# Half-size block products (Strassen's scheme) in the second MLP product of two batches

## The chip, the cores and the metric

The kernel runs on one core of a Trainium2 chip. A core has five engines with a queue of instructions each: TensorE (matrix products, PE in the profile; its weight loads are listed as PEld), VectorE (DVE), ScalarE (ACT), GpSimd (POOL) and SyncE (SP, which here only issues DMA transfers). The queues run side by side and wait for each other by semaphores. Operands lie in SBUF, matrix products arrive in PSUM, and DMA moves data from and to HBM. The metric is the device time in microseconds (us), as the median of several runs.

## The reference

The first half is block-sparse attention over 4 batches, 8 heads, 768 tokens and 64 numbers per head; a boolean mask by blocks of 32 tokens says which scores count. The second half mixes the tokens and ends in an MLP, both with residual paths:

```python
attn = softmax(where(mask, q @ k.T / 8, -1e9));  x = attn @ v      # then [b, 768, 512]
a1 = alpha1 * x + beta1
tok = np.einsum('ts,bsd->btd', w_tok, a1)
u = x + lam * tok
a2 = alpha2 * u + beta2
ch = np.maximum(a2 @ w_ch1, 0.0) @ w_ch2      # 512 -> 2048 -> 512
return u + lam * ch
```

The change concerns the product with `w_ch2`, 768 x 2048 by 2048 x 512 in each batch, and the addition after it.

## The kernel before, in words

The work is done in 16 pairs of heads, four to a batch. Tokens lie six to a partition, so a batch has six token tiles of 128, and `x_sbs[b]` (128 partitions x 6 x 512, float32, three buffers) holds a batch's attention output and later its residual sum `u`. `lam` is folded into the weights beforehand: into `w2b`, the bfloat16 copy of `w_ch2` (16 tiles of 128 rows, 512 columns), by the products on line 764.

PSUM has eight banks: two `sp` tiles of two banks each, three `mm` tiles of one bank, one `op` tile. Scores go to `sp` tiles or to two `mm` tiles (`emit_qk`, L582), ScalarE takes their exponential (`emit_exp`, L600), VectorE multiplies by the mask (`emit_keep`, L617), TensorE forms the products with the values in `op` (L629, L652), and VectorE divides by the row sums (`emit_finish`, L669 and L670). `emit_a1pp` (L686, L687) applies `alpha1` and `beta1`, on GpSimd, for a batch's last head on VectorE. For every two pairs of heads `job_tok2` mixes the tokens (three jobs of 12 matmuls, L826, each followed by the residual addition on L838 and two casts to `ubf` on L844). `emit_udma` transposes `ubf` by DMA, issued on SyncE, and `emit_uscale` (L877) writes `uT`, with `alpha2` and `beta2`, which is what the MLP reads.

The MLP has two kinds of jobs. `job_f1(b, c, n)` makes one 128-wide tile `n` of the 2048 hidden numbers for half `c` of a batch's tokens: four matmuls of 384 columns (L891) into an `mm` tile and a ReLU on ScalarE (L898) into `hts[(b, c)]`. There are 32 in a batch, and `hts` has two buffers. `job_f2(b, o, g)` is a quarter of the second product for token tile `o`: four matmuls of 512 columns (L910) into the `mm` tile `chs[(b, o)]`; the fourth quarter is followed by the addition of `x_sbs` on VectorE into a tile `ot` (L919) and by a store on SyncE's queue. The last token tile of the last batch is done apart, by `job_f2_cols` (matmuls on L930, additions on L938), in a part of 384 and one of 128 columns.

The order of the instructions on each engine is written out by hand. After 45 steps of a first loop, which follows the due times in `PLAN`, come rows of `WEAVE`, counted on from row 15, and each of their letters issues one thing: `q` the scores of three units and the first exponential, `x` a further exponential, `k` a mask product, `p` a group of value products, `0 1 2` what `PLAN` has for the three steps, `L` loads, `Q K Y` transposes and copies for the next pair, `s` the start of a finished pair, `T` one `job_tok2`, `d` one `emit_udma`, `v` one `emit_uscale`, `f` one `job_f1`, `g` one `job_f2`. The nine rows of `W1` are rows 15 to 23; the twelve rows of `W2` are used twice, as rows 24 to 35 and 36 to 47; the three rows of `W3` have no scores left and finish batches 2 and 3. A batch's second product is spread over the rows in which the next batch's scores are computed. Every engine takes its instructions in the order in which they were issued, so what is issued later on a queue waits for what stands before it there.

Of the kernel before, what the change touches and what calls it, by code (L numbers as in the profile page):

```python
# [25 lines left out]
DM = 512  # L26
P = 128
NT = S // P
NH = 4 * DM // P
# [13 lines left out]
W1 = [  # L43
# [9 lines left out]
]  # L53
W2 = [
# [12 lines left out]
]  # L67
W3 = [
# [3 lines left out]
]  # L72
WEAVE = W1 + W2 * (B - 2) + W3
ENG = {
    "kT0": 0,
    "kT1": 0,
# [153 lines left out]
def kernel(  # L230
# [16 lines left out]
    nc = tc.nc  # L247
# [22 lines left out]
    ap_ = ctx.enter_context(tc.tile_pool(name="attn", bufs=1))  # L270
# [4 lines left out]
    def ptile(shape, dt, name):  # L275
        return pp.tile(shape, dt, name=name, tag=name)
# [46 lines left out]
    qTs = [ptile([P, 2, S], BF, f"qTs{i}") for i in range(NQB // 2)]  # L323
    kTs = [ptile([P, 2, S], BF, f"kTs{i}") for i in range(NQB // 2)]
# [24 lines left out]
    for n, src in enumerate((moe_lam, moe_alpha1, moe_beta1)):  # L349
# [10 lines left out]
        out=identb[:],  # L360
# [33 lines left out]
    for o in (slice(0, 4), slice(4, NT)):  # L394
# [18 lines left out]
        out=mbs[0:NBLK, :],  # L413
        in0=mbm[0:NBLK, :],
# [27 lines left out]
    def sp_tile():  # L442
        return psum.tile([P, 2, 512], FP, name="sp", tag="sp", bufs=2)
# [6 lines left out]
    def mm_tile(shape=(P, DM), dt=FP):  # L450
        return psum.tile(list(shape), dt, name="mm", tag="mm", bufs=3)
# [103 lines left out]
    x_sbs = {}  # L555
# [142 lines left out]
    w2b = ptile([P, NH, DM], BF, "w2b")  # L698
# [94 lines left out]
    hts = {}  # L793
# [92 lines left out]
    def job_f1(b, c, n):  # L886
        if n == 0:
            hts[(b, c)] = ap_.tile([P, NH, QC], BF, name="hts", tag="hts", bufs=2)
        ps = mm_tile()
        for dk in range(4):  # L890
            nc.tensor.matmul(  # L891
                ps[:, 0:QC],
                w1b[:, dk, ts(n, P)],
                uTs[b][:, dk, ts(c, QC)],
                start=(dk == 0),
                stop=(dk == 3),
            )
        nc.scalar.activation(  # L898
            hts[(b, c)][:, n, :], ps[:, 0:QC], AF.Relu
        )  # L900

    chs = {}

    def job_f2(b, o, g):
        if g == 0:
            chs[(b, o)] = mm_tile()
        ps = chs[(b, o)]
        ht = hts[(b, o // 3)]
        for nk in range(4 * g, 4 * g + 4):
            nc.tensor.matmul(  # L910
                ps[:],
                ht[:, nk, ts(o % 3, P)],
                w2b[:, nk, :],
                start=(nk == 0),
                stop=(nk == NH - 1),
            )
        if g == 3:
            ot = ap_.tile([P, DM], FP, name="ot", tag="ot", bufs=3)
            nc.vector.tensor_tensor(  # L919
                out=ot[:], in0=x_sbs[b][:, o, :], in1=ps[:], op=ALU.add  # L920
            )
            nc.sync.dma_start(
                out[b].rearrange("(p o) n -> p o n", o=NT)[:, o, :], ot[:]
            )

    def job_f2_cols(b, o, sl):
        ps = mm_tile()
        ht = hts[(b, o // 3)]
        for nk in range(NH):
            nc.tensor.matmul(  # L930
                ps[:, sl],
                ht[:, nk, ts(o % 3, P)],
                w2b[:, nk, sl],
                start=(nk == 0),
                stop=(nk == NH - 1),
            )
        ot = ap_.tile([P, DM], FP, name="ot", tag="ot", bufs=3)
        nc.vector.tensor_tensor(  # L938
            out=ot[:, sl], in0=x_sbs[b][:, o, sl], in1=ps[:, sl], op=ALU.add
        )  # L940
        nc.sync.dma_start(
            out[b].rearrange("(p o) n -> p o n", o=NT)[:, o, sl], ot[:, sl]
        )

    NPAIR = B * NP
    WIDE = [
# [28 lines left out]
    ]  # L975
    N1 = MP * len(WIDE)
    LAG = 2
    todo = {"f": [], "g": [], "t": []}

    def start_mlp(b):  # L980
        todo["f"] += [
            lambda c=c, n=n: job_f1(b, c, n) for c in range(2) for n in range(NH)
        ]
        os_ = range(NT) if b < B - 1 else range(NT - 1)
        todo["g"] += [lambda o=o, g=g: job_f2(b, o, g) for o in os_ for g in range(4)]
# [112 lines left out]
    for s in range(N1):  # L1098
# [42 lines left out]
    def token(t, p):  # L1141
# [34 lines left out]
    assert not (todo["f"] or todo["g"] or todo["t"] or pend or kept)  # L1176
    for sl in (slice(0, 3 * P), slice(3 * P, DM)):
        job_f2_cols(B - 1, NT - 1, sl)
# [1 line left out]
_INS = ['q', 'k', 'v', 'sampled_blocks', 'moe_alpha1', 'moe_beta1', 'moe_w_tok', 'moe_alpha2', 'moe_beta2', 'moe_w_ch1', 'moe_w_ch2', 'moe_lam']  # L1180
_OUTS = [((4, 768, 512), 'float32')]
# [25 lines left out]
```

## Time and profile before

| | us |
|---|---|
| median of three runs (lowest to highest) | 302.34 (302.17 to 303.07) |
| span of the profiled execution, from its first to its last instruction | 300.1 |
| busy in it: TensorE / ScalarE / VectorE / GpSimd | 293.2 / 212.7 / 195.6 / 112.0 |
| ReLU products (L891, 512 matmuls) / second MLP product (L910, 343 recorded), busy | 92.6 / 84.4 |

The profile gives one execution; apart from its span no time of its own is listed, so the difference to the median, 2.2 us, lies around the span or between executions. Busy times of matmuls overlap in its groups, since one starts before the one before it has left the array: the mean length of one in a group is longer than the interval at which they follow each other. A row of a group reads: line, engine, operation, output <- inputs, partitions x elements and type, how many; then busy us and the mean in ns of one; then the idle time of the engine just before them and what ended most of it. A row of the timeline reads: start, length, engine, line, operation, and in square brackets a wait before it with what ended it. Rows of a line's instructions give shortest/mean/longest in ns and the time of the first and the last.

### The profile page before, as it was taken

To read this page: it belongs to the slowest core of one execution; us is meant where nothing else is said; L and a number is where in the kernel's file an instruction comes from. 1 tells how busy PE (TensorE), PEld (TensorE's weight loads), DVE (VectorE), ACT (ScalarE), POOL (GpSimd) and SP (SyncE) were. 2 spreads that over 40 slices of the span, in tenths; PEclk is the share of its full clock that TensorE was granted. 3 is DMA by queue.
4 is the path that set the end of the run, shared out by engine and by line. 5 is a ranking of instruction groups with operands and counts; after the bars stand their busy time and mean duration, and the time that the engine had idled before them with its cause. 6 is when DMAs were issued, how large, how long until landed. Compare 5 with 4: busy or idle time off the path is not lost.

```text
span 300.1 us, 7192 instructions
## 1 busy us (share of the span) xinstructions
PE 293.2 (98%) x2970; PEld 183.2 (61%) x2995; DVE 195.6 (65%) x374; ACT 212.7 (71%) x314; POOL 112.0 (37%) x151
## 2 busy tenths in 40 slices
PE   7999999999999999999999999999999999999996
PEld 2788888664577565555675565565576564555543
DVE  4979899985688796963669687972769672000012
ACT  5999999998899944998878763998779400673210
POOL 8997887632525700564315320362322200000000
PEclk9999999999999999999999999999999999999999
DMA  6999999951491993629835693629102004000011
GB/s 182 187 201 187 189 166 196 194 94 28 101 171 21 142 178 81 131 46 149 127 57 86 110 176 85 120 64 135 49 18 52 37 35 122 37 0 37 35 70 70
DMA packets 57929, 31.26 MB, mean 104 GB/s; under 512 B 37989, under 2 KB 54673, under 8 KB 57897
## 3 DMA queue, kind: packets, MB, share of 16 engines
q0 software_dynamic: 16752, 14.22, 33.1%
q1 hardware_dynamic: 40820, 16.19, 26.3%
q8 instruction: 23, 0.38, 0.5%
q10 hardware_dynamic: 324, 0.40, 0.5%
q14 instruction: 10, 0.07, 0.1%
HBM read 29.75 MB, written 6.29 MB: 120 GB/s over the span
## 4 chain that ended last, share of the span: by engine, by line
PE 94%; ACT 3%; DMA 1%; issue 1%; DVE 0%; ACTq 0%
PE mm L891 28%; PE mm L910 26%; PE sp L582 10%; PE op L652 9%; PE mm L826 8%; PE mm L582 4%; PE mm L802 3%; ACT eT L600 2%; PE op L629 2%; PE mm L629 1%; PE mm L930 1%; DMA ms<-ms_c 1%; PE mm L780 1%; PE mm L492 1%; PE mm L532 0%
## 5 line engine op out<-in xcount | busy, mean ns | idle before, releaser
L600 ACT ACTIVATE eT<-sp,expb 128x1024 f16<-128x1024 f32 x111 | 118.3, 1121 | 1.8 <-PE sp L582 1.1
L891 PE MATMUL mm<-uT,w1b 128*128 128x384 bf16 x512 | 92.6, 326 | 0.1
L898 ACT ACTIVATE hts<-mm 128x384 bf16<-128x384 f32 x128 | 60.9, 500 | 42.1 <-PE mm L891 41.5
L617 DVE TENSOR_TENSOR eT<-eT,mask 128x1024 f16<-128x1024 f16 x99 | 80.2, 840 | 15.9 <-ACT eT L600 15.7
L910 PE MATMUL mm<-w2b,hts 128*128 128x512 bf16 x343 | 84.4, 379 | 1.3 <-issue 0.3
L686 POOL TENSOR_TENSOR a1pp<-x_sb,vbc 128x384 bf16<-128x384 f32 x26 | 29.7, 1141 | 124.2 <-DVE x_sb L670 94.7
L891 PEld LDWEIGHTS <-w1b 128*128 128x128 bf16 x512 | 48.2, 98 | 33.3 <-issue 2.1
L600 ACT ACTIVATE eT<-mm,expb 128x512 f16<-128x512 f32 x66 | 41.8, 685 | 27.2 <-PE mm L582 26.8
L910 PEld LDWEIGHTS <-hts 128*128 128x128 bf16 x368 | 33.7, 98 | 38.4 <-issue 4.7
L919 DVE TENSOR_TENSOR ot<-x_sb,mm 128x512 f32<-128x512 f32 x23 | 15.8, 686 | 49.2 <-PE mm L910 41.8
L652 PEld LDWEIGHTS <-eT 128*128 128x128 f16 x792 | 29.9, 98 | 8.3 <-issue 1.3
L652 PE MATMUL op<-vext,eT 128*128 128x65 f16 x792 | 32.1, 194 | 0.2
L687 POOL TENSOR_TENSOR a1pp<-a1pp,vbc 128x384 bf16<-128x384 bf16 x26 | 27.7, 1065 | 2.1
L582 PE MATMUL sp<-qTs,kTs 88*128 88x512 bf16 (+1 forms) x120 | 26.9, 326 | 1.3 <-ACT kTs L432 0.8
L826 PE MATMUL mm<-a1pp,wtokT 128*128 128x256 bf16 x216 | 25.9, 273 | 0.0
L826 PEld LDWEIGHTS <-wtokT 128*128 128x128 bf16 x216 | 20.6, 98 | 5.5 <-issue 2.5
L582 PE MATMUL sp<-qhT,khT 64*128 64x256 bf16 (+1 forms) x176 | 19.7, 322 | 0.0
L838 DVE TENSOR_TENSOR x_sb<-x_sb,mm 128x512 f32<-128x512 f32 x18 | 12.3, 686 | 10.2 <-PE mm L826 10.1
L582 PEld LDWEIGHTS <-khT 64*128 64x128 bf16 x264 | 10.5, 94 | 12.2 <-issue 8.6
L629 PEld LDWEIGHTS <-eT 128*128 128x128 f16 x360 | 14.9, 97 | 3.8 <-issue 0.3
L670 DVE TENSOR_TENSOR x_sb<-op,rcp 128x384 f32<-128x384 f32 x28 | 15.6, 558 | 1.0
L844 DVE CAST ubf<-x_sb 128x256 bf16<-128x256 f32 (+1 forms) x44 | 13.7, 346 | 0.9
(94 smaller groups left out, 221.8 us busy)
## 6 DMA issues: line engine op xcount, KB each, us to landing
out_dram<-ot SPq DMA_DIRECT2D x23, 256.0 KB
qpad<-in_q_dram POOLq DMA_DIRECT2D x15, 192.0 KB, 4.8
kr<-in_k_dram POOLq DMA_DIRECT2D x15, 192.0 KB, 5.5
vr<-in_v_dram POOLq DMA_DIRECT2D x15, 192.0 KB, 6.1
w1b<-in_moe_w_ch_dram POOLq DMA_DIRECT2D x4, 512.0 KB, 9.1
w2b<-in_moe_w_ch_dram POOLq DMA_DIRECT2D x4, 512.0 KB, 8.1
hts<-in_moe_w_tok_dram POOLq DMA_DIRECT2D x2, 576.0 KB, 9.7
x_sb<-in_k_dram ACTq DMA_DIRECT2D x2, 192.0 KB
```

The lines of the kernel that those rows point to most:

```text
L582: nc.tensor.matmul(sp[jj][:, dst], lhsT, rhs, start=True, stop=True, skip_group_check=True,)
L600: nc.scalar.activation(dst, at, AF.Exp, bias=expb[:], scale=SCALE)
L617: nc.vector.tensor_mul(out=e, in0=e, in1=keep)
L629: nc.tensor.matmul(op[0][:, o, :], ets[u][:, jj, h * QB + n * P : h * QB + n * P + P], vexts[i % NVB][:, w, 2 * jp + jj, :], start=op[1] == 0,
L652: nc.tensor.matmul(op[0][:, o, :], ets[u][:, jj, h * QB + n * P : h * QB + n * P + P], vexts[i % NVB][:, w, 2 * jp + jj, :], start=op[1] == 0,
L686: eng.tensor_tensor(out=dst, in0=x_sbs[b][:, :, cols], in1=bc[0], op=ALU.mult)
L687: eng.tensor_tensor(out=dst, in0=dst, in1=bc[1], op=ALU.add)
L826: nc.tensor.matmul(ps[:, o], wtokT[:, os_, ts(2 * n + o, P)], a1pps[i][:, os_, :], start=(os_ == 0 and o == 0), stop=(os_ == NT - 1 and o ...
L891: nc.tensor.matmul(ps[:, 0:QC], w1b[:, dk, ts(n, P)], uTs[b][:, dk, ts(c, QC)], start=(dk == 0), stop=(dk == 3),)
L898: nc.scalar.activation(hts[(b, c)][:, n, :], ps[:, 0:QC], AF.Relu)
L910: nc.tensor.matmul(ps[:], ht[:, nk, ts(o % 3, P)], w2b[:, nk, :], start=(nk == 0), stop=(nk == NH - 1),)
L919: nc.vector.tensor_tensor(out=ot[:], in0=x_sbs[b][:, o, :], in1=ps[:], op=ALU.add)
```

## The change

In batches 2 and 3 (`STR`) the second product takes token tiles in pairs (t, t+3), t from 0 to 2, one from each half `hts[(b, 0)]` and `hts[(b, 1)]`. The 256 x 2048 by 2048 x 512 product is cut into two by two blocks: two token tiles by two halves of the hidden numbers (`HN` = 8 tiles each), and two halves of `w2b`'s rows by two halves of its columns (`HC` = 256). In the Strassen-Winograd form, four sums of blocks on each side give seven products instead of eight. Each product `job_p(b, t, n)` is 8 matmuls of 256 columns (L1052 of the changed file), 56 for a pair where there were 32 of 512.

The sums on the weights' side (`T1`, `T2`, `T4`, and a fourth written over `w2b`'s own upper right block) are formed once, by 16 instructions of 512 elements on GpSimd (`job_t`, letter `A`, L979); they lie in the four tiles `qTs` and `kTs`, which the later pairs of heads no longer use. The sums on the tokens' side (`job_s`, letter `S`, L1026) are formed for each pair: `X1` and `X2` into new tiles, two more over blocks of `hts`. In batch 2 numbers 1 and 2 run on VectorE and 3 and 4 on GpSimd; in batch 3, 1 to 3 run on VectorE and 4 on GpSimd.

The sums on the results' side are formed partly by accumulation in PSUM (products that go on in a bank in which an earlier one stands) and partly on VectorE, which adds a bank to `x_sb` in place (`plus`, L1062) after a product, sometimes to two blocks at once (`twice`). For a pair, products 6, 7, 5 and 4 use the two banks of one `sp` tile, and product 1 (batch 3) or 6 (batch 2) opens it; products 1, 2 and 3 use `mm` tiles as well. Stores now read `x_sb`, in batches 0 and 1 too, and the tile `ot` and `job_f2_cols` are gone; the last product of all is done in two parts of 128 columns.

Batch 2's products 1 and 2 of the three pairs stand in rows 42, 43 and 46; its products 6, 7, 5, 4, 3 follow from row 47 into `W3`. For that, two of batch 2's `f` are issued earlier (rows 43 and 44). In batch 3 all 32 `f` come first, with the upper and the lower half of the hidden tiles in turn, and its 21 products stand at the very end.

```diff
-WEAVE = W1 + W2 * (B - 2) + W3
+W2L = [
...
+    "q k 0 f x f p s f f x 1 L p k 2 f f f k Y f A A",
+    "q f L f 0 f k 1 f Y x f p g x f p f g k k 2 A A",
+    "q x k x k Q 0 g 1 s f f g p 2 p f f k p f A A",
+    "q T 0 k f 1 x k f T x f 2 p k K p f",
+    "q x 0 x T k 1 k f 2 k f Q f d p L",
+    "q x 0 x K k g d k s f f 1 k p p g 2",
+    "q Y x x S S k g k 0 1 S k S 2 p g v g v",
+]
 W3 = [
...
+    "S S p p p g s g S S S S T T T g g d d v g g S S g g g v g g g f f f f",
+    "f f f f f f f f f f f f",
+    "f f f f f f f f S S S f f S S S f f S S S f f f f",
+    "S S g S g S g g g S S g S g S g g g S S g S g g g g g S g g g g g",
 ]
+STR = (2, 3)
+HN = NH // 2
+HC = DM // 2
+WEAVE = W1 + W2 + W2L + W3
...
+            x = x_sbs[b][:, o, :]
+            nc.vector.tensor_tensor(out=x, in0=x, in1=ps[:], op=ALU.add)
+            emit_store(b, o, slice(0, DM))
...
+    T_ORDER = (
+        ("T1", (1, 2), (1, 1)),
+        ("T2", (2, 2), "T1"),
+        ("T4", (2, 1), "T2"),
+        ((1, 2), (2, 2), (1, 2)),
+    )
...
+    SOP = {
+        1: ("X1", "21", "22", ALU.add),
+        2: ("X2", "X1", "11", ALU.subtract),
+        3: ("21", "11", "21", ALU.subtract),
+        4: ("12", "12", "X2", ALU.subtract),
+    }
...
+    SPLIT = {2: 3, 3: 4}
+    PROD = {
+        1: ("11", (1, 1), 0),
+        2: ("12", (2, 1), 0),
+        3: ("12", (2, 2), 4),
+        4: ("22", "T4", 0),
+        5: ("X1", "T1", 1),
+        6: ("X2", "T2", 2),
+        7: ("21", (1, 2), 3),
+    }
...
+    def plus(x, ps):
+        nc.vector.tensor_tensor(out=x, in0=x, in1=ps, op=ALU.add)
...
+    def job_p(b, t, n):
...
+        if n == 1 or (n == 6 and not tail):
+            if n == 1 and not tail:
+                banks[(b, t)] = [mm_tile()[:]]
+            else:
+                sp = sp_tile()
+                banks[(b, t)] = [sp[:, 0], sp[:, 1]]
+        bk = banks[(b, t)]
+        if n == (2 if tail else 3):
+            bk.append(mm_tile()[:])
...
+        elif n == 2:
+            ps = bk[2] if tail else bk[0]
+            mul(b, t, 2, ps[:, lo], tail)
...
+        elif n == 6:
+            mul(b, t, 6, bk[0][:, lo], not tail)
+            plus(x[:, t + 3, lo], bk[0][:, lo])
+        elif n == 7:
+            mul(b, t, 7, bk[1][:, lo], True)
+            plus(x[:, t + 3, hi], bk[1][:, lo])
+        elif n == 5:
+            mul(b, t, 5, bk[0][:, lo], False)
+            plus(x[:, t : t + 4 : 3, hi], twice(bk[0][:, lo]))
+        elif n == 4:
+            mul(b, t, 4, bk[1][:, lo], False)
+            plus(x[:, t + 3, lo], bk[1][:, lo])
+            emit_store(b, t + 3, slice(0, DM))
+        elif last:
+            for h in range(2):
+                sl = slice(HC + h * P, HC + h * P + P)
+                mul(b, t, 3, bk[2][:, sl], False, ts(h, P))
+                plus(x[:, t, sl], bk[2][:, sl])
+                emit_store(b, t, sl)
...
+    REST = (6, 7, 5, 4, 3)
+    P_ORDER = {
+        2: [(t, n) for t in range(3) for n in (1, 2)]
+        + [(t, n) for t in range(3) for n in REST],
+        3: [(t, n) for t in range(2) for n in (1, 2)]
+        + [(t, n) for t in range(2) for n in REST]
+        + [(2, n) for n in (1, 2) + REST],
+    }
...
+    todo["A"] = [lambda t=t, n=n: job_t(*t, n) for t in T_ORDER for n in range(0, HN, 2)]
...
-    for sl in (slice(0, 3 * P), slice(3 * P, DM)):
-        job_f2_cols(B - 1, NT - 1, sl)
```

More of the change, by code (lines that the diff above doesn't have):

```diff
@@ L900, in job_f1 @@
         )
+        did.add(("f", b, c, n))
     chs = {}
@@ new lines, with a_of, job_s @@
+    xs = {}
+    def a_of(b, t, name, r=slice(0, HN)):
+        if name in ("X1", "X2"):
+            return xs[(b, t, name)][:, r]
+        c, half = {"11": (0, 0), "12": (0, 1), "21": (1, 0), "22": (1, 1)}[name]
+        return hts[(b, c)][:, HN * half + r.start : HN * half + r.stop, ts(t, P)]
+    SOP = {
[4 more added lines that the diff above has]
+    }
+    def job_s(b, t, n, r=slice(0, HN)):
+        dst, a, c, op = SOP[n]
+        rows = range(r.start, r.stop)
+        for name in (a, c):
+            if name[0] == "X":
+                assert all(("S", b, t, int(name[1]), m) in did for m in rows)
+            else:
+                h, half = divmod(int(name) - 11, 10)
+                assert all(("f", b, h, HN * half + m) in did for m in rows)
+        if n == 3:
+            assert all(("S", b, t, 1, m) in did for m in rows)
+        if n == 4:
+            assert (b, t, 2) in did
+        if dst[0] == "X" and (b, t, dst) not in xs:
+            tag, bufs = ("eT", 6) if b == B - 1 else ("xs", 4)
+            xs[(b, t, dst)] = ap_.tile([P, HN, P], BF, name="xs", tag=tag, bufs=bufs)
+        eng = nc.gpsimd if n >= SPLIT[b] else nc.vector
+        eng.tensor_tensor(
+            out=a_of(b, t, dst, r), in0=a_of(b, t, a, r), in1=a_of(b, t, c, r), op=op
+        )
+        did.update(("S", b, t, n, m) for m in rows)
@@ new lines, with mul @@
+    SPLIT = {2: 3, 3: 4}
[8 more added lines that the diff above has]
+    }
+    banks = {}
+    def mul(b, t, n, ps, start, cols=slice(0, HC)):
+        a, m, need = PROD[n]
+        if need:
+            assert all(("S", b, t, need, r) in did for r in range(HN))
+        c, half = {"1": (0, 0), "X": (1, 0)}.get(a[0], (1, 0))
+        if need == 0:
+            h, half = divmod(int(a) - 11, 10)
+            assert all(("f", b, h, HN * half + r) in did for r in range(HN))
+        for r in range(HN):
+            nc.tensor.matmul(
+                ps,
+                a_of(b, t, a)[:, r],
+                b_row(m, r)[:, cols],
+                start=(start and r == 0),
+                stop=(r == HN - 1),
+                skip_group_check=True,
+            )
```

114 lines of the change are left out of this document (83 added, 31 removed), and 8 rows, old and new, of tables (W2L, W3).

## The prediction, made before the changed kernel was run

> **What bounds the kernel now.** I read the page first: engine shares, the slices, the chain that ended last.
>
> ```profile
> PE 293.2 (98%) x2970; PEld 183.2 (61%) x2995; DVE 195.6 (65%) x374; ACT 212.7 (71%) x314; POOL 112.0 (37%) x151
> ...
> PEclk9999999999999999999999999999999999999999
> ...
> PE 94%; ACT 3%; DMA 1%; issue 1%; DVE 0%; ACTq 0%
> ```
>
> TensorE is occupied in every slice at the full granted clock and makes up 94% of the chain. A busy TensorE is not yet one at its rate, so next come the chain's pieces, for what a matmul takes in a stream:
>
> ```profile
> 84.99 1.31 PE mm L826 x12
> ...
> 113.95 1.73 PE mm L910 x8
> ```
>
> A 512-wide matmul costs 1.73/8 = 0.216 us and a 256-wide one 1.31/12 = 0.109, half, with a new weight tile each. So the stream goes by columns, and the weight loads hide. Every microsecond TensorE waits now is a microsecond of the end; hence the waits view matters for what is absent from it: no matmul is listed there as waiting for VectorE. The windows over the last stages:
>
> ```profile
> 4.00:6.00 2.00, 0.99 (x10) 0.41 (x8) 1.88 (x8) 1.22 (x7) 1.81 (x4) 1.00 0.87 272
> ...
> 233.19:255.49 22.30, 22.04 (x167) 12.81 (x170) 12.84 (x26) 4.15 (x6) 2.08 (x2) 1.00 0.21 65
> 255.49:276.30 20.81, 20.76 (x123) 11.93 (x122) 1.37 (x2) 12.71 (x26) 0.00 (x0) 1.00 0.07 26
> 276.30:297.06 20.76, 20.65 (x116) 10.76 (x116) 3.31 (x5) 3.03 (x7) 0.00 (x0) 1.00 0.13 51
> ```
>
> Columns after the length: TensorE, weight loads, VectorE, ScalarE, GpSimd. From 233 us on TensorE lacks 0.4 us in 64, and VectorE does little in the last 42.
>
> **The change, part by part.** *The stream.* A pair of token tiles cost 2 x 16 x 0.216 = 6.92 us and now costs 7 x 8 x 0.109 = 6.12 (0.874 a product). Six pairs gain 4.8 us if TensorE never waits.
>
> *Round trips.* In the built order of the changed kernel, waits stand per PSUM tile, not per bank. Products 6, 7, 5, 4 of a pair share one two-bank `sp` tile, and the first matmul of each waits for VectorE's addition of the one before, even where that addition reads the other bank (7 after 6, 5 after 7, 4 after 5). Prices:
>
> ```profile
> L826 PE MATMUL mm<-a1pp,wtokT 128*128 128x256 bf16 x216 | 25.9, 273 | 0.0
> ...
> L919 DVE TENSOR_TENSOR ot<-x_sb,mm 128x512 f32<-128x512 f32 x23 | 15.8, 686 | 49.2 <-PE mm L910 41.8 <-remote 5.4 <-PE mm L891 1.1
> ...
> L938 DVE TENSOR_TENSOR ot<-x_sb,mm 128x384 f32<-128x384 f32 x1 | 0.6, 553 | 1.9 <-PE mm L930 1.9
> ...
> L938 DVE TENSOR_TENSOR ot<-x_sb,mm 128x128 f32<-128x128 f32 x1 | 0.3, 289 | 0.3 <-PE mm L930 0.3
> ```
>
> The timeline shows the handovers (start, length, engine):
>
> ```profile
> 292.53 1.03 PE L910 MATMUL mm<-w2b,hts 128*128 128x512 bf16 x4
> ...
> 293.60 0.69 DVE L919 TENSOR_TENSOR ot<-x_sb,mm 128x512 f32<-128x512 f32 x1 [2.76 <-PE mm L910]
> ...
> 6.63 1.11 ACT L600 ACTIVATE eT<-sp,expb 128x1024 f16<-128x1024 f32 x1 [0.21 <-PE sp L582]
> ...
> 7.80 0.60 PE L582 MATMUL sp<-qTs,kTs 88*128 88x256 bf16 x4 [0.33 <-ACT eT L600]
> ```
>
> The last matmul of a product ends 0.273 after its start, 0.164 after the next could have started. VectorE begins 0.04 after a matmul's end (292.53 + 1.03 to 293.60). A 256-wide addition lies between 0.289 and 0.553: 0.42, the middle. TensorE resumes 0.06 after its releaser (6.63 + 1.11 to 7.80; ScalarE there). A round trip through a 256-wide addition thus costs 0.164 + 0.04 + 0.42 + 0.06 = 0.68 us, through the 512-wide one after product 5 0.95; a whole pair 2.3.
>
> *Batch 3.* Its products run last, with nothing between them: 3 x 2.3 = 6.9. The second 128-wide half of the very last product waits for the addition of the first (one tile): 0.163 + 0.04 + 0.29 + 0.06 = 0.55. Sum 7.4; the 21 products are 2.4 of the stream's gain, so this tail grows by 5.0. VectorE's pre-sums there (128x512, two 16-bit inputs) fit beside the next product:
>
> ```profile
> L764 DVE TENSOR_TENSOR w2b<-w2b,lam_bcb x16: 411/418/1133, 49.4 to 72.8; 128x512 bf16<-128x512 bf16 x16
> ...
> L617 DVE TENSOR_TENSOR eT<-eT,mask x99: 677/686/1496, 58.4 to 236.9; 128x1024 f16<-128x1024 f16 x99
> ...
> L687 POOL TENSOR_TENSOR a1pp<-a1pp,vbc x26: 910/951/1253, 18.3 to 239.6; 128x384 bf16<-128x384 bf16 x26
> ```
>
> Two take 0.84 against 0.87 for a product plus its drain: nothing, but 0.4 each if they stretch to 1.13. Product 3 waits for GpSimd's sum; by 951 ns per 384 elements, 1024 take at most 2.5 us (3.3 by the longest), and four products lie between: hidden. ScalarE's ReLUs are as before.
>
> *Batch 2 from its pair 0 to the first ReLU product of batch 3.* Here VectorE, GpSimd and ScalarE stand in the path, so I follow the queues. Now:
>
> ```profile
> 233.42 0.59 PE L582 MATMUL sp<-qhT,khT 64*128 64x512 bf16 x4
> ...
> 234.77 2.12 ACT L600 ACTIVATE eT<-sp,expb 128x1024 f16<-128x1024 f32 x2
> ...
> 235.62 1.99 DVE L617 TENSOR_TENSOR eT<-eT,mask 128x1024 f16<-128x1024 f16 x3
> ...
> 237.53 0.19 DVE L669 RECIPROCAL rcp<-op 128x6 f32<-128x6 f32 x1
> 237.76 0.56 DVE L670 TENSOR_TENSOR x_sb<-op,rcp 128x384 f32<-128x384 f32 x1
> ...
> 238.40 1.17 POOL L686 TENSOR_TENSOR a1pp<-x_sb,vbc 128x384 bf16<-128x384 f32 x1 [6.79 <-DVE x_sb L670]
> ...
> 241.14 0.56 DVE L687 TENSOR_TENSOR a1pp<-a1pp,vbc 128x384 bf16<-128x384 bf16 x1
> ...
> 241.90 4.09 PE L826 MATMUL mm<-a1pp,wtokT 128*128 128x256 bf16 x36
> ...
> 244.72 0.69 DVE L838 TENSOR_TENSOR x_sb<-x_sb,mm 128x512 f32<-128x512 f32 x1
> 245.45 0.50 DVE L844 CAST ubf<-x_sb 128x256 bf16<-128x256 f32 x2
> ...
> 246.76 0.49 DVE L844 CAST ubf<-x_sb 128x256 bf16<-128x256 f32 x2
> ...
> 249.83 0.48 DVE L877 TENSOR_SCALAR uT<-uraw,ab2T 128x768 bf16<-128x768 bf16 x1 [2.58 <-DMA uraw<-ubf]
> ```
>
> Clocked from the last scores (233.19), the token mixing starts at 8.7 and the first ReLU product at 22.3. After the change, in us from the same point, every instruction at the duration above and VectorE strictly in its built order:
>
> Product 6 takes an `sp` tile that the scores hold until their exp ends, 234.77 + 1.06 - 233.19 = 2.6; TensorE, out of work at 0.8, waits 1.9 (its first wait on ScalarE of that length). Product 6 runs 2.7 to 3.6, its addition 3.8 to 4.2, product 7 4.3 to 5.1. VectorE goes on with two mask products to 5.6 and reciprocal and scaling to 6.4, and only then does addition 7, to 6.8: product 5 waits from 5.1 to 6.9. Addition 5 ends at 8.7, a uT scaling at 9.2, pair 1's two 128x1024 pre-sums (0.69 each, L617's form) at 10.6, reciprocal and scaling of the last head at 11.4, its two `a1pp` steps at 12.5. TensorE has long done products 4 and 3 and the value products (10.5) and starts the mixing at 12.6. GpSimd is not late: its two sums of pair 0 (2.5 each) end at 6.3, its own `a1pp` at 8.5.
>
> The mixing ends at 16.5, product 6 of pair 1 at 17.4. VectorE still owes additions 4 and 3 (13.4), pair 2's pre-sums (14.8) and three times residual add and casts (1.2 each, 18.4) before addition 6 (18.8): product 7 starts at 18.9, after 1.5 of waiting. The nine products from there take 7.9, and five round trips (5, 4 of pair 1; 7, 5, 4 of pair 2) 2 x 0.95 + 3 x 0.68 = 3.9: the ReLU products start at 30.7. That is 8.4 later than now. The transposes are issued at 18.4 (one store more than now stands before them on SyncE, its addition done at 13.4) and land 2.6 later as now (249.83 after 246.76 + 0.49), so uT is whole long before 30.7.
>
> *Rows 42 to 46.* Six products and 32 ReLU jobs stand before those scores in place of seven 512-wide jobs and 30 ReLU jobs: 5.2 + 1.3 - 6.1 = +0.5. Product 2 of each pair accumulates into what two additions (256 and 512 wide, 1.1) read after product 1. Other matmuls lie between (1.7, 1.3 and 2.0 us), but VectorE comes late:
>
> ```profile
> 211.50 1.04 PE L910 MATMUL mm<-w2b,hts 128*128 128x512 bf16 x4
> ...
> 212.47 1.70 DVE L617 TENSOR_TENSOR eT<-eT,mask 128x1024 f16<-128x1024 f16 x2 [0.34 <-ACT eT L600]
> ```
>
> Pair 1's additions stand behind these mask products: from 214.17, with 1.1 until 215.3, while TensorE is ready at 211.50 + 0.87 + 1.30 = 213.7: 1.6, and 1.9 with the 1.5 of earlier additions partly in front of the masks. Pairs 0 and 2 by the same look: 0.2 and 0.3. Together 2.4 (bounds 0, if ScalarE's lead lets VectorE run ahead, and 4).
>
> *The rest.* 16 weight differences (512 elements, 1.2 to 1.7 us each by L687) go to GpSimd, idle enough in rows 36 to 43. Their price is what they do to VectorE: L617 runs from 677 to 1496 ns, the long ones where GpSimd works. The Trainium skill, "SBUF — State Buffer", section Who interferes with whom, has it that a VectorE instruction with two SBUF inputs contends with a GpSimd one that reads SBUF; the rows agree. I take 0, since TensorE waits for no mask product there now, and 3 as the upper end. ReLU jobs two rows earlier: 0, ScalarE pauses later in the same rows; if not, 1.0 (two ReLUs). Stores that read `x_sb`: 0, three buffers, and batch 0's is stored some eight rows before batch 3 writes it; else one store's latency.
>
> Sum: rows 42 to 46 0.5 + 2.4, the queue stage 8.4, the tail 5.0: +16.3 us (the stream's gain of 4.8 is within the stages). Profiled span 300.1; the median of the runs, 302.34, is 2.2 above it, which I keep as what lies around the span. 302.3 + 16.3 = 318.6, said as 318.5.
>
> **The rivals.** *VectorE's order matters less:* round trips alone (6.9 + 0.55 in the tail, 3.9 + 0.7 + 0.7 before it), the exp wait of 1.9, and nothing of the queues; with the stream's 4.8 that is +9.9, 312. For: VectorE is used 12.84 in 22.30 us; a late TensorE gives it time. It decides if product 5 of pair 0 starts within 0.7 of product 7's end. *Contention is worse:* ten mask products and pre-sums beside GpSimd's six long sums stretch by up to 0.8 each, half of it on the path: +4, 323. *Faster:* the additions hide beside the next product, whose first matmul starts before they end. Then the stream alone counts: 302.3 - 4.8 = 297.5. Against it stand the built waits; for it nothing but the banks, which differ. *The clock drops:* in the tail TensorE would work 18.4 of 26 us in pieces of 0.9. At half clock 36 products of 0.874 and 32 ReLU jobs of 0.65 cost another 52 us at most, 370. Against: in 4 to 6 us it was busy 0.99 of 2.00 at clock 1.00. The Trainium skill, "TensorE: Matmul & The Clock Gate", section A second HAM failure mode, tells of a kernel whose short pauses at PSUM made the gate swing; by that rule it would be this case, and the 4 to 6 us row speaks against it, though over two microseconds only.
>
> **How the numbers follow.** Forecast 0.66 (314 to 322 alone), VectorE's order less 0.17, contention 0.11, clock 0.03, faster 0.03. The range 310 to 324 takes in the first three but for their edges and leaves out the rest. About 0.3% (0.9 us) is what a measurement here can tell from no change. Faster 0.03 is that rival; same 0.01; slower 0.96, the others.
>
> **What would show it.** Right: the waits view lists TensorE waiting for the additions, 15 to 20 times; the last 26 us show TensorE near 70%; products of 0.87 us with 0.7 or 0.95 between them; one wait near 1.9 on an exp; the mixing about 4 us and the ReLU products about 8 later after the last scores. Wrong: products back to back, additions of 0.3, a granted clock under 1.00, the sums on GpSimd over 3 us, a new wait in rows 36 to 41, or fewer matmul columns than counted.

## The result, and the profile after

The changed kernel takes 340.3 us (median of four runs, 339.31 to 341.39) against 302.25 us before in the same comparison: a ratio of 1.126, with a 95% interval of 1.123 to 1.129. It is slower by 38 us where 16.3 were forecast; 340.3 lies above the range of 310 to 324. The profiled execution took 339.3 us, the fastest of the four, with a span of 337.6. One run of a later variant took 337.8 us at a granted clock of 0.85 where its other eleven took 302 to 303; it is left out of the ratio given for that variant.

The page of the changed kernel, engine shares, three rows of the slices and the shares of the chain:

```profile
PE 300.8 (89%) x3115; PEld 200.3 (59%) x3131; DVE 240.9 (71%) x429; ACT 212.5 (63%) x314; POOL 155.4 (46%) x176
...
PE   7999999999999999999999968959966657999674
...
DVE  4979998957878797367789898774799853005652
...
PEclk9999999999999999999999999989997778999999
...
PE 69%; DVE 18%; DMA 4%; ACT 4%; issue 2%; POOL 2%; SPq 0%; POOLq 0%; DVEq 0%
```

TensorE has fallen from 98% to 89%, VectorE has gone from nothing to 18% of the chain, and two places show a granted clock under full speed. The holes in TensorE's row begin at the 24th slice, from 194 us, which is not the tail but row 40. So I cut both traces at the same places: the start of row 36's scores, of row 43's, of row 47's, the first ReLU products of batch 3, and the end. The windows of the kernel before (row 47's stage, 233.19 to 255.49, stands in the prediction), then of the changed one (after the length: busy time of TensorE, weight loads, VectorE, ScalarE and GpSimd, granted clock, DMA):

```profile
169.98:210.75 40.77, 40.51 (x405) 23.94 (x410) 29.16 (x53) 30.84 (x47) 13.83 (x15) 1.00 0.60 107
210.75:233.19 22.44, 22.34 (x231) 14.46 (x234) 16.27 (x27) 18.04 (x28) 6.24 (x6) 1.00 0.18 40
...
255.49:300.10 44.61, 41.41 (x238) 22.69 (x238) 4.97 (x8) 15.74 (x32) 0.00 (x0) 1.00 0.11 42
```

```profile
170.65:218.27 47.62, 41.46 (x414) 24.59 (x418) 41.16 (x53) 31.01 (x47) 30.47 (x27) 1.00 0.59 96
218.27:247.33 29.06, 25.09 (x253) 17.14 (x253) 20.61 (x33) 18.74 (x30) 11.55 (x10) 0.94 0.07 15
247.33:287.53 40.20, 26.40 (x214) 20.20 (x214) 29.02 (x44) 3.27 (x4) 16.83 (x8) 0.83 0.12 37
287.53:337.60 50.07, 40.77 (x305) 28.94 (x302) 17.68 (x39) 15.68 (x32) 6.35 (x3) 1.00 0.12 43
```

| stage | before | forecast | after |
|---|---|---|---|
| rows 36 to 42 | 40.8 | 66.1 together with the next | 47.6 |
| rows 43 to 46 | 22.4 | | 29.1 |
| row 47 to batch 3's first ReLU product | 22.3 | 30.7 | 40.2 |
| from there to the end | 44.6 | 49.6 | 50.1 |

The cut ahead of the last stage lies 0.16 us behind the start of the first ReLU matmul, before and after. The tail came out as forecast. The miss lies in the first three stages, and there VectorE's busy time says where: with the same 53 VectorE instructions in the first of them, 41.2 us in place of 29.2. Rows of the changed kernel's timeline, in row 40 and in row 43:

```profile
195.88 2.82 POOL L979 TENSOR_TENSOR kTs<-w2b,qTs 128x512 bf16<-128x512 bf16 x2
196.06 3.19 DVE L635 TENSOR_TENSOR eT<-eT,mask 128x1024 f16<-128x1024 f16 x2
...
200.00 0.91 PE L670 MATMUL op<-vext,eT 128*128 128x65 f16 x24 [2.84 <-DVE x_sb L688]
...
225.00 1.03 PE L1052 MATMUL mm<-w2b,hts 128*128 128x256 bf16 x8 [3.62 <-DVE x_sb L1062]
```

Beside two weight differences on GpSimd two mask products take 3.19 us, 1.6 each. The next head's value products need the `op` bank, which VectorE empties behind them (L688), and TensorE stands for 2.84 us. In row 43 product 2 waits 3.62 us for additions that are queued behind four mask products, which take 5.3 us together. In row 47's stage the same happens beside batch 2's pre-sums on GpSimd, 1024 elements each:

```profile
248.54 2.62 POOL L1026 TENSOR_TENSOR hts<-hts 128x1024 bf16<-128x1024 bf16 x1 [2.37 <-DVE xs L1026]
...
249.10 2.61 DVE L635 TENSOR_TENSOR eT<-eT,mask 128x1024 f16<-128x1024 f16 x1
...
261.35 2.42 POOL L1026 TENSOR_TENSOR hts<-hts,xs 128x1024 bf16<-128x1024 bf16 x1
261.84 2.35 DVE L705 TENSOR_TENSOR a1pp<-a1pp,vbc 128x384 bf16<-128x384 bf16 x1
...
267.10 0.69 DVE L856 TENSOR_TENSOR x_sb<-x_sb,mm 128x512 f32<-128x512 f32 x1 [0.92 <-PE mm L844]
267.82 2.62 DVE L862 CAST ubf<-x_sb 128x256 bf16<-128x256 f32 x2
...
273.08 1.14 PE L1052 MATMUL sp<-w2b,hts 128*128 128x256 bf16 x8 [2.51 <-DVE x_sb L1062]
...
274.73 1.86 PE L1052 MATMUL sp<-qTs,xs 128*128 128x256 bf16 x8 [0.51 <-DVE x_sb L1062]
```

A mask product lasts 2.61 us in place of 0.69, a scaling step 2.35 in place of 0.56, a pair of casts 2.62 in place of 0.5 when it stands beside one of these sums; the residual addition between them, with one operand in PSUM, keeps its 0.69. And the product at 274.73 lasts 1.86 us, not 1.03: the clock was halved. No matmul of these stages is listed as waiting for a result of GpSimd; what they wait for is VectorE, and twice ScalarE's exponential.

### The profile page after: what moved, and what is told of

The parts are those of the page before. It is cut to its first block, busy times and chain, and to the rows that moved or that the text cites. A ratio compares the mean times of both kernels' runs of the same rounds, so it can differ in the third digit from the quotient of the medians.

```text
span 337.6 us, 7553 instructions
## 1 busy us (share of the span) xinstructions
PE 300.8 (89%) x3115; PEld 200.3 (59%) x3131; DVE 240.9 (71%) x429; ACT 212.5 (63%) x314; POOL 155.4 (46%) x176
## 3 DMA queue, kind: packets, MB, share of 16 engines
q0 software_dynamic: 16752, 14.22, 29.1%
## 4 chain that ended last, share of the span: by engine, by line
PE 69%; DVE 18%; DMA 4%; ACT 4%; issue 2%; POOL 2%; SPq 0%; POOLq 0%; DVEq 0%
PE mm L909 19%; PE mm L929 10%; PE sp L600 8%; PE sp L1052 7%; DVE eT L635 7%; PE mm L844 6%; PE op L670 5%; DVE x_sb L1062 4%; ACT eT L618 3%; PE mm L1052 3%; PE mm L820 2%; PE mm L600 2%; PE op L647 2%; DVE ubf L862 2%; DMA uraw<-ubf 1%
## 5 line engine op out<-in xcount | busy, mean ns | idle before, releaser
L635 DVE TENSOR_TENSOR eT<-eT,mask 128x1024 f16<-128x1024 f16 x99 | 93.8, 980 | 13.2 <-ACT eT L618 13.0
L704 POOL TENSOR_TENSOR a1pp<-x_sb,vbc 128x384 bf16<-128x384 f32 x26 | 29.1, 1121 | 111.6 <-DVE x_sb L688 86.3
L618 ACT ACTIVATE eT<-mm,expb 128x512 f16<-128x512 f32 x66 | 41.7, 684 | 28.2 <-PE mm L600 27.9
L929 PE MATMUL mm<-w2b,hts 128*128 128x512 bf16 x176 | 44.6, 380 | 0.8 <-issue 0.2
L670 PEld LDWEIGHTS <-eT 128*128 128x128 f16 x792 | 31.2, 100 | 12.9 <-DVE x_sb L688 5.0
L1026 POOL TENSOR_TENSOR hts<-hts,xs 128x1024 bf16<-128x1024 bf16 x6 | 13.5, 2251 | 53.0 <-DVE x_sb L1062 40.0
L670 PE MATMUL op<-vext,eT 128*128 128x65 f16 x792 | 33.7, 197 | 4.5 <-DVE x_sb L688 4.2
L1052 PEld LDWEIGHTS <-hts 128*128 128x128 bf16 x248 | 24.4, 102 | 21.3 <-issue 17.5
L844 PE MATMUL mm<-a1pp,wtokT 128*128 128x256 bf16 x216 | 27.3, 282 | 4.1 <-DVE a1pp L705 2.9
L929 PEld LDWEIGHTS <-hts 128*128 128x128 bf16 x192 | 16.9, 98 | 19.4 <-issue 3.6
L1062 DVE TENSOR_TENSOR x_sb<-x_sb,sp 128x256 f32<-128x256 f32 (+1 forms) x27 | 12.9, 478 | 17.4 <-PE sp L1052 17.4
L1052 PE MATMUL mm<-w2b,hts 128*128 128x256 bf16 (+1 forms) x128 | 16.6, 274 | 4.6 <-DVE x_sb L1062 4.6
```

Of the source, the lines that this page charges most:

```text
L618: nc.scalar.activation(dst, at, AF.Exp, bias=expb[:], scale=SCALE)
L635: nc.vector.tensor_mul(out=e, in0=e, in1=keep)
L670: nc.tensor.matmul(op[0][:, o, :], ets[u][:, jj, h * QB + n * P : h * QB + n * P + P], vexts[i % NVB][:, w, 2 * jp + jj, :], start=op[1] == 0,
L704: eng.tensor_tensor(out=dst, in0=x_sbs[b][:, :, cols], in1=bc[0], op=ALU.mult)
L844: nc.tensor.matmul(ps[:, o], wtokT[:, os_, ts(2 * n + o, P)], a1pps[i][:, os_, :], start=(os_ == 0 and o == 0), stop=(os_ == NT - 1 and o ...
L929: nc.tensor.matmul(ps[:], ht[:, nk, ts(o % 3, P)], w2b[:, nk, :], start=(nk == 0), stop=(nk == NH - 1),)
```

## The experiments

Two theories stood against each other. Theory G: GpSimd's instructions with two inputs stretch VectorE's, VectorE becomes the bound, and the pauses that follow cost clock too. Theory V: VectorE is late by its order and by the waits on PSUM tiles, and the stretch fills time in which it would have idled. All variants but the last three were run once, and the four executions of the changed kernel differ by 2 us among themselves (339.31 to 341.39), so a total is good to 1 or 2 us and the windows are read first.

**Without the weight differences.**

```diff
-    todo["A"] = [lambda t=t, n=n: job_t(*t, n) for t in T_ORDER for n in range(0, HN, 2)]
+    todo["A"] = [lambda t=t: nc.gpsimd.memset(t[:], 0.0) for t in tpool]
-WEAVE = W1 + W2 + W2L + W3
+WEAVE = W1 + [r + " A" if 4 <= i < 8 else r for i, r in enumerate(W2)] + W2L + W3
```

> Left out: the 16 weight differences on GpSimd in rows 36 to 43; the four tiles that hold them are filled with zeros earlier (rows 28 to 31), so products 4 to 7 of batches 2 and 3 work on other data, at the same length. Theory G (GpSimd's two-input instructions stretch VectorE's, and VectorE becomes the bound): the mask products of these rows go back to 0.69 to 0.85 us, the start of row 43's scores comes 6 to 7 us earlier than in the changed kernel (near 41 us after row 36's instead of 47.6), row 43 itself loses another 3 to 5, and the total is 327 to 331 us against 340.3. Theory V (VectorE is late by its order and by the waits on PSUM tiles; the stretch only fills time in which it would idle): at most 2 us less, 338 or more.

Measured: 329.9 us, 10.4 less than the changed kernel's median. Its windows from row 36 and from row 43, which are 6.5 and 3.8 us shorter than there:

```profile
170.40:211.57 41.17, 40.90 (x413) 24.69 (x418) 29.39 (x53) 30.84 (x47) 13.55 (x15) 1.00 0.64 111
211.57:236.80 25.23, 23.30 (x253) 16.32 (x254) 17.62 (x33) 18.77 (x30) 6.18 (x6) 1.00 0.09 17
```

The 33 mask products of these rows in the changed kernel, and without the differences (the groups of these stretches):

```profile
L635 DVE TENSOR_TENSOR eT<-eT,mask 128x1024 f16<-128x1024 f16 x33 | 36.9, 1157 | 3.1 <-ACT eT L618 3.1
```

```profile
L635 DVE TENSOR_TENSOR eT<-eT,mask 128x1024 f16<-128x1024 f16 x33 | 26.0, 823 | 5.1 <-ACT eT L618 5.1
```

VectorE's time in the first stage is back at 29.4, the stage at 41.2 us, and the second has 25.2 where the forecast's 2.9 us of late additions and jobs would make 25.3. Theory V allowed 2 us.

**Batch 2's pre-sums on VectorE.**

```diff
-    SPLIT = {2: 3, 3: 4}
+    SPLIT = {2: 5, 3: 4}
```

> Batch 2's pre-sums 3 and 4 go from GpSimd to VectorE, six instructions of 1024 elements at about 0.69 us; nothing else is changed. Theory G: in the stage from row 47's scores to batch 3's first ReLU product (40.2 us in the changed kernel) the mask products go back from 1.1 to 2.6 us to 0.7, the last head's scaling steps from 1.66 and 2.35 to 0.56, a pair of casts from 2.6 to 0.5; that is some 10 us off VectorE against 4 added, and shorter pauses keep the clock up: the stage takes 30 to 35 us, the total 330 to 335. Theory V: VectorE has 4 us more in front of the additions that TensorE waits for; the stage takes 42 to 45 us and the total is 342 to 345.

Measured: 331.0 us, 9.3 less, with row 47's stage at 31.9 us, 8.3 less:

```profile
247.13:279.04 31.91, 20.79 (x214) 17.04 (x213) 23.86 (x50) 3.27 (x4) 1.91 (x2) 1.00 0.16 46
```

VectorE has six instructions more in that stage and is busy 5 us less, 23.9 in place of 29.0, and the clock is 1.00. Theory V, by which more work on VectorE makes it worse, falls.

**Both.**

> The two first experiments together: the 16 weight differences left out (zeros stand in their tiles), batch 2's pre-sums 3 and 4 on VectorE. What is left is the change without GpSimd work beside VectorE's. If the two prices only add up, 329.9 + 331.0 - 340.3 = 320.6; the prediction's sum without any contention was 318.5. If one had hidden the other (the queue of VectorE late in any case): 324 or more.

Measured: 322.2 us. The windows from row 36, 43, 47, and from the first ReLU product:

```profile
171.56:213.18 41.62, 40.92 (x414) 24.71 (x418) 29.39 (x53) 30.85 (x47) 13.55 (x15) 1.00 0.65 109
213.18:238.41 25.23, 23.30 (x255) 16.31 (x254) 17.62 (x33) 18.77 (x30) 6.17 (x6) 1.00 0.09 17
238.41:270.33 31.92, 20.79 (x214) 17.03 (x213) 23.87 (x50) 3.28 (x4) 1.92 (x2) 1.00 0.16 46
270.33:320.50 50.17, 40.92 (x306) 29.04 (x303) 17.67 (x39) 15.73 (x32) 6.45 (x3) 0.99 0.12 43
```

The prices add up: the three stages are 18.1 us shorter than in the changed kernel, where the two changes by themselves took 10.3 and 8.3 off them. The total, 322.2, is 1.6 above the 320.6 of the plain sum; 0.9 of it lies ahead of row 36 (171.56 against 170.65), and the rest is within what single runs differ by. For the same matmuls (883 and 881 recorded), TensorE is busy 7.9 us less in the three stages than in the changed kernel, where the clock was at 0.50 for part of them. So of the 18.1 us at most some 7.9 are the half clock; how much of that would have been hidden in waits is not shown.

**Batch 2's pre-sums on GpSimd, in quarters.**

```diff
+        step = 2 if b == 2 and n >= SPLIT[b] else r.stop - r.start
+        for m in range(r.start, r.stop, step):
+            s = slice(m, m + step)
+            eng.tensor_tensor(
+                out=a_of(b, t, dst, s), in0=a_of(b, t, a, s), in1=a_of(b, t, c, s), op=op
+            )
```

> Batch 2's pre-sums 3 and 4 stay on GpSimd, each cut into four instructions of 256 elements in place of one of 1024. If a VectorE instruction with two SBUF inputs waits for the GpSimd instruction that is running to end (2.25 to 2.62 us now): the mask products of row 47's stage take 1.1 to 1.4 us instead of 2.3 to 2.6, the stage 34 to 37 us instead of 40.2, the total is 334 to 337. If it is GpSimd's whole work that takes VectorE's time, cut as it may be: within 1.5 us of 340.3.

Measured: 338.5 us, the stage at 38.8. VectorE's rows in it:

```profile
249.62 1.16 DVE L635 TENSOR_TENSOR eT<-eT,mask 128x1024 f16<-128x1024 f16 x1
...
261.06 0.90 DVE L705 TENSOR_TENSOR a1pp<-a1pp,vbc 128x384 bf16<-128x384 bf16 x1
...
265.38 1.35 DVE L862 CAST ubf<-x_sb 128x256 bf16<-128x256 f32 x2
```

Half of this came true. The mask product goes from 2.61 to 1.16 us, the scaling step from 2.35 to 0.90, the casts from 2.62 to 1.35: what one VectorE instruction loses goes with the length of the GpSimd instruction beside it. The time did not follow, only 1.4 us of the stage, and 338.5 us lies between what was expected by either reading. A pre-sum in quarters keeps GpSimd busy longer, 2.7 to 3.6 us instead of 2.2 to 2.6, and so stands beside more instructions: all three pairs of casts now take 1.35, where one took 2.62 and two 0.5. The mixing starts 14.2 us after row 47's scores in place of 16.9, but product 7 of pair 1 then waits 4.06 us for VectorE, and the clock is at 0.50 for the ten us from there.

**TensorE kept busy in two pauses.**

```diff
+            if p == N1 // 3 + len(WEAVE) - 4 and len(todo["t"]) == 3:
+                emit_warm(13)
...
+            if b == 2 and t == 1:
+                emit_warm(12)
```

> Added: 25 matmuls of 512 columns whose result nobody reads (0.216 us each), 13 ahead of the last token mixing and 12 ahead of product 7 of batch 2's pair 1, where TensorE waits 2.87 and 2.51 us in the changed kernel. Nothing else moves. If the pauses of TensorE are what halves the granted clock afterwards (0.50 at 264 to 267 us and at 274 to 280.7): the clock stays at 1.00 from 260 to 287, the mixing takes 4 instead of 5.5 us and products 5, 4 and 3 of that pair 0.87 instead of 1.65 to 1.86; 3 to 5 us less, 335.5 to 337.5. If the clock falls for another reason: no gain, 340 to 342, and still rows of 0.50.

Measured: 336.7 us, 3.6 below the changed kernel's median and 2.6 below its fastest run. Windows of the changed kernel, first TensorE alone at half clock, then nine us around its products from product 7 of pair 1 on; and nine us around the same products in this run:

```profile
274.00:280.00 6.00, 4.71 (x23) 0.50 0.31 59
...
273.00:282.00 9.00, 7.39 (x40) 5.02 (x40) 2.66 (x7) 0.00 (x0) 0.00 (x0) 0.62 0.31 75
```

```profile
272.00:281.00 9.00, 5.94 (x49) 4.72 (x49) 4.01 (x11) 0.00 (x0) 0.00 (x0) 1.00 0.38 102
```

In nine us 40 matmuls stand there and 49 here, none of them among the added ones, and the mixing takes 4.10 us in place of 5.45. So it is the pauses that bring the half clock in these two places. What it is worth is less than the totals say: from row 47's scores to the first ReLU product this run takes 38.3 us where the profiled execution of the changed kernel takes 40.0 (to the start of the ReLU matmul), and of the 2.9 us between the two spans 1.2 lie ahead of row 47, where nothing was added yet.

**The tail in another order.**

```diff
-        + [(t, n) for t in range(2) for n in REST]
-        + [(2, n) for n in (1, 2) + REST],
+        + [(t, n) for n in (6, 7, 5, 4) for t in range(2)]
+        + [(2, 1), (2, 2), (0, 3), (2, 6), (1, 3), (2, 7), (2, 5), (2, 4), (2, 3)],
```

The pre-sums of pairs 1 and 2 move along with them in the last row of `W3`.

> Batch 3's products in another order: pairs 0 and 1 take turns in products 6, 7, 5, 4, each on its own two-bank tile, and their products 3 stand between those of pair 2. If the round trips are what the tail lacks (0.68 us each, 0.95 after product 5, as the prediction had it): the first two pairs lose theirs, 2 x 2.3, and pair 2 two of its four, some 1.4; the tail from the first product on goes from 29.3 us to about 23.5, the total to 334 to 335. If VectorE's work limits the tail (it is busy 14.2 of 29.3 us there, in products of 0.87 with an addition of 0.42 to 0.69 and a pre-sum each): less than 2 us, 338 or more.

Measured: 334.3 us. The total meets the expectation, but not for its reason: from the first product (306.22) to the end (332.6) it is 26.4 us in place of 29.3, half of what was expected, and row 47's stage happened to be 1.7 shorter in this execution. The rows that hold the other half:

```profile
308.36 2.12 POOL L1026 TENSOR_TENSOR hts<-hts,xs 128x1024 bf16<-128x1024 bf16 x1 [37.48 <-DVE x_sb L1062]
308.41 2.35 DVE L1026 TENSOR_TENSOR xs<-hts 128x512 bf16<-128x512 bf16 x1
...
311.61 0.60 PE L1052 MATMUL sp<-qTs,xs 128*128 128x256 bf16 x4 [0.86 <-DVE x_sb L1062]
...
314.15 1.91 PE L1052 MATMUL sp<-w2b,hts 128*128 128x256 bf16 x16 [1.51 <-DVE x_sb L1062]
```

Pre-sum 4 on GpSimd stretches a pre-sum on VectorE from 0.42 to 2.35 us, and the additions come late behind it; the two waits of 0.86 and 1.51 us are 2.4 of the missing 2.9. In the last variant below all pre-sums are on VectorE and no two neighbouring products share a tile; there no matmul of the tail is listed as waiting for an addition, and it is 22.5 us from the first product to the end.

**Batch 3 alone, and where its weight differences stand.** Batch 2 is as before the change (rows 36 to 47 and the first row of `W3` too); all pre-sums are on VectorE; the products of the three pairs take turns on the two `sp` tiles; the differences are emitted among the ReLU jobs, and the second half of the very last product has a tile of its own. The main lines of the edit:

```diff
-STR = (2, 3)
+STR = (3,)
...
-    "f f f f f f f f f f f f",
+    "A A A A A A A A A A A A A A A A f f f f f f f f f f f f",
...
-    SPLIT = {2: 3, 3: 4}
+    SPLIT = {3: 5}
...
+        3: [(int(p) // 10, int(p) % 10) for p in (
+            "1 2 6 11 7 12 5 16 4 17 21 15 26 14 27 22 25 3 24 13 23".split())],
...
+                ps = mm_tile()[:] if h else bk[2]
```

> Batches 0 to 2 as in the kernel before (rows 36 to 47 and the first row of W3 as there, stores from x_sb). Batch 3 alone takes the seven products, all 16 weight differences stand on GpSimd among its ReLU jobs, where VectorE and GpSimd had nothing to do, all pre-sums on VectorE; the 21 products are ordered so that two neighbours never use one two-bank tile, and the last half has a tile of its own. By theory G and the round trips as measured: three pairs gain 2.4 us, products after a 512-wide addition lose 0.1 each, the end from the last product on is as before: 300 to 301, against 302.4 before. If TensorE still waits for VectorE in the tail (its own 15 us in 18.4): 302 or more.

Measured: 302.42 us against 301.95, a ratio of 1.0017 (1.0008 to 1.0026): no gain. From the first ReLU product to the end it is 1.5 us shorter than before (43.3 against 44.8), but row 47's stage is 1.8 longer (23.9 against 22.1, both up to the start of that product). GpSimd, held by nothing, ran the differences from 241 us on, beside the last scaling steps:

```profile
241.07 5.12 POOL L966 TENSOR_TENSOR qTs<-w2b 128x512 bf16<-128x512 bf16 x4
241.10 1.53 DVE L691 TENSOR_TENSOR a1pp<-x_sb,vbc 128x384 bf16<-128x384 f32 x1
...
244.21 4.09 PE L831 MATMUL mm<-a1pp,wtokT 128*128 128x256 bf16 x36 [1.58 <-DVE a1pp L692]
```

The same kernel with 12 of the differences at the ends of rows 36 to 41, as the changed kernel has them:

> The same kernel with 12 of the 16 weight differences moved to the ends of rows 36 to 41, where the changed kernel has them, and the last 4 where they were. No product of batch 2 and no pre-sum waits there. Theory G: mask products beside them 1.4 to 1.6 us, VectorE becomes the bound in these rows: 5 to 7 us longer than the run beside it, 305 to 308. Theory V: TensorE waits for no mask product there, at most 1 us.

Measured: 307.02 us, 1.0173 (1.0156 to 1.0190), so 5.1 us more than before and 4.6 more than the variant beside it. In the profiled execution, the slowest of the four (308.06), row 43's scores start 47.1 us after row 36's (40.8 before, 41.2 in the variant beside it, 47.6 in the changed kernel): the differences alone, with no product or pre-sum of batch 2 about, make nearly all of that stage's loss. Theory V gave 1 us at most. Last, GpSimd held until `uT` is whole (an `A` more stands in the row for it):

```diff
-    todo["A"] = [lambda t=t, n=n: job_t(*t, n) for t in T_ORDER for n in range(0, HN, 2)]
+    todo["A"] = [
+        lambda: nc.gpsimd.tensor_copy(out=gate[:], in_=uTs[B - 1][:, 3, 0:1])
+    ] + [lambda t=t, n=n: job_t(*t, n) for t in T_ORDER for n in range(0, HN, 2)]
```

> As batch3_only, but GpSimd first waits for the last tile of batch 3's uT (it copies one number of it) before it begins the weight differences; in batch3_only nothing held them, and they ran from 241 to 260 us beside the last scaling steps, casts and uT scalings. If those stretched VectorE instructions are what ate the gain (TensorE waited 1.6 us for the last scaling step): the first ReLU product of batch 3 comes 1.6 us earlier, the total is 300.3 to 301.2 against 302.0 before. If the differences are then late for the products (16 of about 1.17 us, 18.7 us, against 20.8 of ReLU jobs), or the gain went elsewhere: 302 or more.

Measured: 301.03 us against 302.21, 0.9956 (0.9943 to 0.9970), 1.2 us faster than the kernel before. Its windows, cut at the times of the kernel before (its own first ReLU product comes at 256.16, its first product at 276.96):

```profile
233.20:255.50 22.30, 22.30 (x170) 12.60 (x168) 13.22 (x27) 4.15 (x6) 3.53 (x5) 1.00 0.22 65
255.50:276.30 20.80, 20.80 (x128) 12.43 (x127) 3.79 (x10) 14.68 (x30) 16.53 (x15) 1.00 0.04 13
276.30:299.50 23.20, 19.62 (x182) 16.82 (x179) 13.98 (x32) 1.04 (x3) 0.00 (x0) 1.00 0.20 69
```

GpSimd's 16.5 us now stand where VectorE does 3.8, and TensorE has no hole in the first two windows.

## Why the prediction was wrong, point by point

**The stream: right.** The chain of the changed kernel at the head of the tail:

```profile
308.33 0.87 PE sp L1052 x8
309.21 0.87 PE mm L1052 x8
```

A product takes 0.87 us, as said. The last experiment shows what three pairs are worth when little waits: 1.2 us at the median, of the 2.4 counted. In its profile TensorE's work from the first ReLU product to the last matmul is 1.9 us shorter than before (39.8 against 41.7); the stretch behind the last matmul is 0.5 longer, and rows 36 to 42 are 0.7 longer in that execution, which is not explained.

**Round trips and the tail: right.** The changed kernel's timeline in the tail:

```profile
321.99 1.03 PE L1052 MATMUL sp<-qTs,xs 128*128 128x256 bf16 x8 [0.51 <-DVE x_sb L1062]
323.06 0.69 DVE L1062 TENSOR_TENSOR x_sb<-x_sb,sp 128x512 f32<-128x512 f32 x1 [0.79 <-PE sp L1052]
323.80 1.03 PE L1052 MATMUL sp<-kTs,hts 128*128 128x256 bf16 x8 [0.78 <-DVE x_sb L1062]
```

A wait of 0.51 behind a 256-wide addition and of 0.78 behind the 512-wide one; with the last matmul's 0.16 that is 0.67 and 0.94, against 0.68 and 0.95. The last stage grew by 5.5, against 5.0. The 0.5 more is one wait, of 1.36 us in place of 0.78: there GpSimd's pre-sum 4 stretches a pre-sum on VectorE from 0.42 to 1.88 us ahead of the addition, for which the prediction had counted nothing. TensorE waits for additions 21 times, against 15 to 20 (the waits view; us in total, times, longest):

```profile
PE sp L1052 <- DVE x_sb L1062: 15.0, 17, 2.8
...
PE mm L1052 <- DVE x_sb L1062: 4.6, 4, 3.6
...
PE sp L1052 <- ACT eT L618: 1.9, 1, 1.9
```

**The queue stage: right without GpSimd's pre-sums.** 31.9 us (in the run with both taken out, with 4.1 us more on VectorE) against 30.7. Its steps fit too: the mixing starts 13.1 us after the scores (12.6 said), product 7 of pair 1 waits 1.93 (1.5 said), and the wait on the exp, the last row above, was 1.9 as said. Rows 36 to 46 lose 41.62 + 25.23 - 63.21 = 3.6 there, against 2.9; product 2 waits 0.33, 1.71 and 0.21 us in the three pairs, where 0.2, 1.9 and 0.3 were said. The steps that were counted make 20 us where 16.3 were said, 1.6 of it before row 36.

**"The rest": the step that failed.** "I take 0, since TensorE waits for no mask product there now, and 3 as the upper end." That was the price of the 16 weight differences for VectorE; they cost 10.4 us. The queue stage had the same step in it: "every instruction at the duration above" takes VectorE's instructions at the length they have with little beside them, while GpSimd's six sums run there, and that cost 9.3 more. Together, 18.1 us of the 38 (the run with both taken out), against 0 in the sum.

The row quoted for the step (677 to 1496 ns) was read as a limit of the mask product's own stretch. But the neighbours it shows are GpSimd's instructions of 384 elements, 0.9 to 1.4 us long. Beside 512 elements a mask product takes 1.6, once 3.12 where two of them follow each other, and beside 1024 it takes 2.6. And that nothing waits for a mask product before the change was no cover: VectorE was used 29.2 of 40.8 us there, 12 us more fill it, and what is late next, the `op` bank and the additions behind the masks, is what TensorE waits for. The waits views, before and after, have it in the weight loads of the value products, where the prediction went by the matmuls alone:

```profile
PEld L652 <- DVE x_sb L670: 0.5, 2, 0.3
```

```profile
PEld L670 <- DVE x_sb L688: 5.0, 2, 3.2
```

Twice they waited for the `op` bank before the change, by 0.3 us at most: it was emptied just in time. The rule of the Trainium skill that stood beside the row of the mask products, from "SBUF — State Buffer", section Who interferes with whom, pointed this way. That page also has it that a VectorE instruction with at most one SBUF input, outside its two-port modes, does not contend; the residual addition's 0.69 us beside a pre-sum agrees.

**The rival "contention is worse": right in kind, too small.** It put 0.8 us on each of ten instructions and half on the path, +4. The pre-sums' price was 9.3 (8.3 in their own stage), with 1.9 us on a mask product, 1.8 on a scaling step and 2.1 on a pair of casts.

**The rival "the clock drops": right in kind, wrong in place.** The prediction placed it in the tail, in pieces of 0.9 us with pauses of 0.5 to 0.8. There the clock stayed at 1.00. It fell at pauses of 2.5 to 3.6 us in the stages ahead of it; when two of them were filled the clock stayed up there, and the stage was 1.7 us shorter. The quoted row from 4 to 6 us had only short pauses, 0.84 us the longest, so it said nothing of long ones. Part of the two prices of GpSimd's work is this, 7.9 us of TensorE's time at most.

## What to carry to other kernels

Before work is moved to an engine that looks idle, ask what runs beside it on the engines that share something with it: here 16 instructions of 1.2 to 1.6 us on GpSimd cost 10.4 us, and the same 16 cost nothing that shows where VectorE had little to do. Take a stretched instruction's longest time as a reading of its neighbour, and expect more from a longer neighbour. A place where nobody waits covers a delay only up to that engine's idle time; work that out first, with the stretch in it.

## What the runs showed of the hardware that was not expected

- A VectorE instruction with two inputs in SBUF, or a cast or scaling, is stretched by the GpSimd instruction with two inputs that runs beside it, the more the longer that one is: a mask product of 0.69 us alone took 1.16 beside sums of 256 elements (0.9 us each), up to 1.6 beside 512 (1.2 to 1.6 us) and 2.6 beside 1024 (2.6 us). One took 3.12, from before the first to after the second of two sums of 512.
- The granted clock goes to 0.50 at pauses of TensorE and stays there for 3 to 10 us. In the changed kernel this followed pauses of 3.62, 2.79, 2.87 and 2.51 us (226 to 229 us, 257 to 260, 264 to 267, 274 to 280), in the run without weight differences one of 1.92 us (241 to 251). Ten pauses of 0.4 to 1.4 us in the 26 us of the tail do nothing. The length alone does not decide it: a pause of 1.93 us in the run with batch 2's pre-sums on VectorE left the clock at 1.00, and of one and the same pause in row 40, 2.84 us in the profile of the changed kernel (at 200 us) and 2.85 in that of batch 3 alone with early differences (at 200.8), the first left it at 1.00 and the second was followed by 0.50. "TensorE: Matmul & The Clock Gate" of the Trainium skill, section What's actually happening, tells of free-running windows of about 3.4 us over which TensorE's activity is judged; by that rule the place of a pause counts too. The runs agree as far as they go, but show no such window itself.
- Matmuls that nobody reads, put where TensorE would wait, can pay: with 25 of them, which take 5.4 us of TensorE, the stage was 1.7 us shorter, by one profiled execution of each.
